# Decode intermediates and gate products move to PSUM, weight sums to GpSimd, one Strassen pair of the first MoE2 group becomes plain, and a softplus is issued later

## The chip, the core and the metric

The kernel runs on one core of one Trainium2 chip. The metric is device time of that core in microseconds (us). PE is the matrix engine (PEld its weight loads), DVE is VectorE, ACT is ScalarE, POOL is GpSimd, SP is the engine whose queue issues the DMAs.

## The reference

Sparse attention over 4 sequences of 576 tokens (8 heads of 64; half of them see the last 32 positions, half every 32nd), then two feed-forward layers over all 2304 tokens of width 512:

```python
def _moe_ref(x, w_gate, w_val, w_out):          # d_ff = 1536
    gate = 1.0 / (1.0 + np.exp(-(x @ w_gate)))
    val = x @ w_val
    return (gate * val @ w_out).astype(np.float32)

def _moe2_ref(x, w_in, w_out):                  # d_ff = 2048
    h = x @ w_in
    g = np.maximum(h, 0.0) + np.log1p(np.exp(-np.abs(h)))   # softplus
    return (g @ w_out).astype(np.float32)
```

The weights arrive as 64-bit floats, and the kernel turns them into pairs of 32-bit numbers itself.

## The kernel before

**Products.** Every 32-bit operand is held as a high and a low part, and `mm3` issues three matmuls (lines 68 to 70) for one product: high by high, high by low, low by high. Tokens lie in five blocks, four of 512 and the last (block 4) of 256. The hidden width is worked off in groups of 256 columns: six for MoE1 (groups 0 to 5), eight for MoE2 (groups 6 to 13).

**MoE1.** `step` does for one group and block: `gates` (two banks `ps_g`, sigmoid by ACT into `sg`), `out1` of the step before (four banks `ps_y`, added by DVE into `acc`, line 300), `values1` (two banks `ps_v`). When a `ps_v` is full, DVE multiplies it by `sg` (line 280), ACT rounds the product into `gh` (line 246) and DVE forms the remainder `gl` (line 247). `gh` and `gl` are what the next `out1` multiplies, and between the last `ps_v` and that `out1` stands only one `gates`.

**Decoding.** In the same steps DVE decodes pieces of 128x512 raw weights: two instructions for the high part `f` (lines 111, 115), one for the power of two `e` (line 121), one for the low word (line 133 or 191), then ACT and POOL split the result. `decode_steps` does it for MoE1's own next weights; `store_in`, `store_out` and `store_sums` do it for MoE2's weights and write them to DRAM, `store_sums` with the four differences and sums (lines 210 to 214) that the Strassen-like products need. A store passes through one of two `pair` buffers; its DMA is put into a list `ready` and issued by a later `send`. A table `plan` deals the pieces over the steps. Three `raw` buffers hold loaded pieces. `soon(n, fn)` runs `fn` after `n` more `tick`s (one per product in MoE1), and every engine works in the order in which the code was written.

**MoE2.** Blocks 0 and 1 form pair 0, blocks 2 and 3 pair 1. `pair_step` multiplies a pair with 7 products (42 matmuls) instead of 8, from operands that `operand_steps` builds of MoE1's result (differences, and their high and low parts, into `xh`/`xl` and weight buffers no longer used). After the first product A11 a copy of its bank (`snap`, line 448, ACT) must be made before A12 may add to that bank. `plain_step` does block 4 without the trick. `softplus` is three ACT instructions (lines 375 to 377), then `finish` on DVE (line 382) and the split again. `downs` are the second-layer products, six matmuls into one `ps_y`, placed between the others by `counts`. PSUM has 8 banks here: 4 for `ps_h`, `ps_g`, `ps_v`, and 4 for `ps_y`.

Of the kernel before, what the change touches and what calls it, by code (L numbers as in the profile page):

```python
# [36 lines left out]
GC = 2  # L37
# [7 lines left out]
def tile_sparse_attention_moe_moe2(  # L45
# [78 lines left out]

    def decode_steps(pools, refill=True):
        (g, m, c), low, high, f, e = fields(pools)
        hi, lo = (x[:, c * PIECE:(c + 1) * PIECE] for x in wset[g % 2][m])
        high_part(high, f)
        yield
        power(f, e)  # L130
        ff, ef = f.bitcast(F32), e.bitcast(F32)
        nc.scalar.activation(out=hi, in_=ff, func=AF.Copy)
        nc.vector.scalar_tensor_tensor(
            out=ef, in0=low, scalar=2.0 ** -52, in1=ef, op0=ALU.mult, op1=ALU.mult
        )
# [6 lines left out]
    ready, halves = [], {}  # L142
# [13 lines left out]
    def send(n=1):  # L156
        for _ in range(min(n, len(ready))):
            dst, src = ready.pop(0)
            nc.sync.dma_start(out=dst, in_=src.bitcast(F32))

    def split_store(pools, src, dst):
        pair = pools["s"].tile([P, 2, 2, HALF], F32R, tag="pair", name="pair")
        h, l = pair[:, :, 0, :], pair[:, :, 1, :]
        nc.scalar.activation(out=h, in_=src, func=AF.Copy)
        nc.gpsimd.tensor_tensor(out=l, in0=src, in1=h.bitcast(F32), op=ALU.subtract)
        ready.append((dst, pair))

    def store_in(pools):
        (g, m, c), low, high, f, e = fields(pools)
        a = pools["q"].tile([P, PIECE], F32, tag=f"a{c}", name=f"a{c}")  # L170
        nc.scalar.activation(out=a, in_=low, func=AF.Copy, scale=2.0 ** -52)
        high_part(high, f)
        yield
        power(f, e)
        load_next()
        send()
        ff, ef = f.bitcast(F32), e.bitcast(F32)
        nc.gpsimd.tensor_tensor(out=a, in0=a, in1=ef, op=ALU.mult)
        nc.gpsimd.tensor_tensor(out=a, in0=a, in1=ff, op=ALU.add)
        halves[c] = a.rearrange("p (k n) -> p k n", k=2)  # L180
        dst = in_s[g - NG1][:, 2 * c:2 * c + 2]
        soon(9, lambda: split_store(pools, halves[c], dst))
        yield

    def store_out(pools):
        (g, m, c), low, high, f, e = fields(pools)
        high_part(high, f)
        yield
        power(f, e)
        ff, ef = f.bitcast(F32), e.bitcast(F32)  # L190
        nc.vector.scalar_tensor_tensor(
            out=ef, in0=low, scalar=2.0 ** -52, in1=ef, op0=ALU.mult, op1=ALU.mult
        )
        load_next()
        send()
# [5 lines left out]
        ready.append((out_s[g - NG1][:, c], pair))  # L201
        yield

    def store_sums(pools, g, part):
# [102 lines left out]
    second = (1, 3)  # L307
    x_ops = {}

    def operand_steps(pair):  # L310
# [16 lines left out]
        def keep(name, k, src, eng):  # L327
            h, l = (x[:, k, :] for x in home[name])
            nc.scalar.activation(out=h, in_=src, func=AF.Copy)
            eng.tensor_tensor(out=l, in0=src, in1=h.bitcast(F32), op=ALU.subtract)  # L330

        for k in range(hk):
            b11, b21 = part(i, k), part(i, hk + k)
            b12, b22 = part(j, k), part(j, hk + k)
            nc.vector.tensor_tensor(out=b11, in0=b12, in1=b11, op=ALU.subtract)
            nc.gpsimd.tensor_tensor(out=b12, in0=b22, in1=b12, op=ALU.subtract)
            keep("T1", k, b11, nc.vector)
            yield
# [32 lines left out]
    def softplus(g, t, c, src, sg, pools, wait=2, last=False):  # L371
# [7 lines left out]
        soon(1, begin) if last else begin()  # L379
# [43 lines left out]
    def pair_step(g, pair, counts, pools, after=None):  # L423
# [52 lines left out]
        softplus(g, j, 0, u2, c12[:, 1, :], pools, wait=3, last=True)  # L476
# [374 lines left out]
    with tc.manual_schedule():  # L851
# [6 lines left out]
            "h": pool("ps_h2", 4, space=PSUM), "y": pool("ps_y2", 4, space=PSUM),  # L858
# [56 lines left out]
        def also(name):  # L915
            if not downs:
                next(work, None)
                next(work, None)

        for g in range(NG1, NG):  # L920
# [6 lines left out]
            first = (2, 2, 2, 2) if g > NG1 else (4, 0, 0, 0)  # L927
            if more:
                pair_step(g, 0, first, pools, also if g == NG1 else None)
                for _ in work:  # L930
                    pass
                if g > NG1:
# [86 lines left out]
```

## Time and profile before

| what | value |
|---|---|
| median of 3 runs | 1008.25 us (1006.47 to 1010.69) |
| the profiled execution | 1006.59 us, of it span 1004.8 us |
| PE busy | 936.6 us (93%) |
| DVE busy | 721.4 us (72%) |
| ACT, POOL busy | 423.2 us (42%), 320.7 us (32%) |
| mean granted PE clock | 0.97 |

Busy time of PE includes matmuls that overlap and those at a lower clock, so 93% does not say that only 7% could be saved. A share over the whole span also hides that attention, MoE1 and MoE2 have different limits; the stages are read apart below.

### The profile page before, as it was taken

The numbers are of one execution on the slowest core, as the hardware profiler recorded it, in microseconds if no ns is written. First come the engines' busy times: TensorE is split into PE (matmuls) and PEld (weight loads), VectorE is DVE, ScalarE is ACT, GpSimd is POOL, SyncE is SP. The second block draws the span as 40 slices with busy tenths as digits, with TensorE's granted clock in tenths as the row PEclk, the third lists the DMA queues.
The fourth block names the chain that finished last, engine by engine and source line by source line (L and its number), as shares of the span: only waits on it lengthen the run. The fifth ranks groups of instructions, "written<-read, shape, count | busy, mean of one in ns | idle before, by whom it ended". The sixth has DMA issues, their size and how long they took to land.

```text
span 1004.8 us, 14179 instructions
## 1 busy us (share of the span) xinstructions
PE 936.6 (93%) x5369; PEld 765.7 (76%) x5369; DVE 721.4 (72%) x1087; ACT 423.2 (42%) x815; POOL 320.7 (32%) x250
## 2 busy tenths in 40 slices
PE   8999999998997998998887996999999999999998
PEld 6777777887785886886675884878787878787886
DVE  7888665388889899889889656656665666565665
ACT  5855545232222221332133446453545454545443
POOL 4545311066555575556478644000000000000000
PEclk9999999999998998999898997999999999999999
DMA  8944321034444445443553401121212121212123
GB/s 222 238 151 141 94 80 43 1 124 129 144 158 139 147 147 167 175 139 126 179 179 142 150 1 32 53 76 51 83 44 84 42 84 43 84 42 84 43 95 136
DMA packets 39123, 107.79 MB, mean 107 GB/s; under 512 B 4752, under 2 KB 5264, under 8 KB 39056
## 3 DMA queue, kind: packets, MB, share of 16 engines
q1 hardware_dynamic: 38624, 106.28, 33.5%
q8 instruction: 42, 0.69, 0.3%
q10 hardware_dynamic: 432, 0.62, 0.2%
q14 instruction: 25, 0.20, 0.1%
HBM read 77.00 MB, written 29.88 MB: 106 GB/s over the span
## 4 chain that ended last, share of the span: by engine, by line
PE 55%; DVE 26%; ACT 10%; issue 7%; DMA 2%; POOL 0%; SPq 0%; ACTq 0%; POOLq 0%; DVEq 0%
PE ps_y L68 9%; PE ps_y L69 9%; PE ps_y L70 9%; DVE f L115 5%; DVE f L111 5%; PE ps_h L68 4%; PE ps_h L70 4%; PE ps_h L69 4%; DVE gl L247 3%; ACT gh L246 3%; DVE acc L300 2%; DVE e L121 2%; PE ps_v L68 2%; PE ps_g L68 2%; PE ps_v L70 2%
## 5 line engine op out<-in xcount | busy, mean ns | idle before, releaser
L246 ACT ACTIVATE gh<-sg 128x512 fp32r<-128x512 f32 (+1 forms) x92 | 51.0, 563 | 172.8 <-DVE sg L280 126.1
L410 DVE TENSOR_TENSOR acc<-ps_y,acc 128x512 f32<-128x512 f32 x126 | 86.1, 689 | 46.4 <-PE ps_y L70 42.5
L68 PE MATMUL ps_y<-o,gh 128*128 128x512 f32 x288 | 114.0, 396 | 0.0
L69 PE MATMUL ps_y<-o,gh 128*128 128x512 f32 x288 | 113.7, 395 | 0.0
L70 PE MATMUL ps_y<-o,gl 128*128 128x512 f32 x288 | 113.4, 394 | 0.0
L247 DVE TENSOR_TENSOR gl<-sg,gh 128x512 fp32r<-128x512 f32 (+1 forms) x92 | 72.7, 790 | 53.5 <-ACT gh L246 53.5
L115 DVE SCALAR_TENSOR_TENSOR f<-raw,f 128x512 uint32<-128x512 uint32 x68 | 81.1, 1192 | 2.3
L300 DVE TENSOR_TENSOR acc<-ps_y,acc 128x512 f32<-128x512 f32 (+1 forms) x100 | 61.0, 629 | 26.1 <-PE ps_y L70 25.9
L375 ACT ACTIVATE cs<-cs 128x512 f32<-128x512 f32 x48 | 30.3, 632 | 95.7 <-DVE cs L429 95.7
L68 PEld LDWEIGHTS ps_y<-o,gh 128*128 128x128 f32 x288 | 55.5, 193 | 11.8
L69 PEld LDWEIGHTS ps_y<-o,gh 128*128 128x128 f32 x288 | 55.3, 192 | 11.8
L70 PEld LDWEIGHTS ps_y<-o,gl 128*128 128x128 f32 x288 | 55.1, 191 | 11.7
L429 DVE TENSOR_TENSOR cs<-ps_h,cs 128x512 f32<-128x512 f32 x80 | 54.9, 686 | 11.6 <-PE ps_h L70 10.1
L68 PE MATMUL ps_y<-gh,w12h 128*128 128x512 f32 (+1 forms) x120 | 48.4, 403 | 15.6 <-ACT gh L246 15.6
L721 POOL TENSOR_TENSOR sm<-sm,st 128x480 f32<-128x480 f32 (+3 forms) x32 | 25.6, 800 | 105.9 <-DVE st L720 59.6
L111 DVE TENSOR_SCALAR f<-raw 128x512 uint32<-128x512 uint32 x68 | 58.5, 861 | 0.8 <-POOL w10l L137 0.8
L68 PE MATMUL ps_h<-xh,A 128*128 128x512 f32 (+1 forms) x128 | 44.6, 349 | 15.0 <-ACT cs L448 15.0
L68 PE MATMUL ps_y<-gh,w02h 128*128 128x512 f32 (+1 forms) x120 | 49.3, 410 | 9.8 <-ACT gh L246 9.8
L382 DVE SCALAR_TENSOR_TENSOR cs<-cs 128x512 f32<-128x512 f32 x48 | 34.1, 710 | 31.6 <-ACT cs L377 31.6
L69 PE MATMUL ps_y<-gl,w12h 128*128 128x512 f32 (+1 forms) x120 | 48.0, 400 | 4.7 <-DVE gl L247 4.6
L247 DVE TENSOR_TENSOR gl<-cs,gh 128x512 fp32r<-128x512 f32 x48 | 33.2, 691 | 26.1 <-ACT gh L246 25.9
L69 PE MATMUL ps_y<-gl,w02h 128*128 128x512 f32 (+1 forms) x120 | 48.1, 401 | 4.0 <-DVE gl L247 4.0
(194 smaller groups left out, 2600.6 us busy)
## 6 DMA issues: line engine op xcount, KB each, us to landing
raw<-in_w_dram SPq DMA_DIRECT2D x68, 512.0 KB, 4.3
in_s<-pair SPq DMA_DIRECT2D x32, 512.0 KB, 5.1
out_s<-pair SPq DMA_DIRECT2D x16, 512.0 KB, 3.9
A<-in_s SPq DMA_DIRECT2D x32, 256.0 KB, 2.8
S<-in_s SPq DMA_DIRECT2D x32, 256.0 KB, 2.7
o<-out_s SPq DMA_DIRECT2D x16, 512.0 KB, 4.3
out_dram<-acc SPq DMA_DIRECT2D x18, 256.0 KB, 2.0
qbuf<-in_q_dram SPq DMA_DIRECT2D x16, 151.0 KB, 3.1
```

The lines of the kernel that those rows point to most:

```text
L68: nc.tensor.matmul(ps, lhsT=lh, rhs=rh, start=first, stop=False, **kw)
L69: nc.tensor.matmul(ps, lhsT=lh, rhs=rl, start=False, stop=False, **kw)
L70: nc.tensor.matmul(ps, lhsT=ll, rhs=rh, start=False, stop=last, **kw)
L111: nc.vector.tensor_scalar(out=f, in0=high, scalar1=3, scalar2=0x3FFFFFFF, op0=ALU.logical_shift_left, op1=ALU.bitwise_and,)
L115: nc.vector.scalar_tensor_tensor(out=f, in0=high, scalar=0xC0000000, in1=f, op0=ALU.bitwise_and, op1=ALU.bitwise_or,)
L246: nc.scalar.activation(out=gh[:, c, 0:n], in_=src, func=AF.Copy)
L247: low = lambda: nc.vector.tensor_tensor(out=gl[:, c, 0:n], in0=src, in1=gh[:, c, 0:n].bitcast(F32), op=ALU.subtract)
L300: nc.vector.tensor_tensor(out=y, in0=ps[:, 0:n], in1=y, op=ALU.add)
L375: nc.scalar.activation(out=sg, in_=src, func=AF.Abs)
L382: nc.vector.scalar_tensor_tensor(out=sg, in0=src, scalar=0.0, in1=sg, op0=ALU.max, op1=ALU.add)
L410: nc.vector.tensor_tensor(out=y, in0=ps, in1=y, op=ALU.add)
L429: nc.vector.tensor_tensor(out=dst, in0=ps, in1=src, op=ALU.add)
```

## The change

Four edits:

- From the end of attention on, the masked word of the high part and the power of two are written to a PSUM bank `ps_x` (one buffer, taken from the `ps_y` banks, which fall from 4 to 3). In `store_in` the power stays in SBUF, because POOL reads it. The gate product overwrites its own bank `ps_v` instead of `sg`, so `gh` and `gl` are made from PSUM.
- `store_sums` runs on POOL. The DMA of a store is issued where its split is written, without `ready` and `send`; the split of the sums comes 6 ticks later instead of 2.
- In MoE2's first group (6) blocks 2 and 3 are done by two `plain_step`s with second-layer products in between. Pair 1's operands are built one piece at a time over that group, in another order, and needed from group 7 on; block 3 therefore needs its whole `xh`/`xl` (`second`).
- The softplus of block 4 starts two ticks (first half) and one tick (second half) later, which is after the next pair's A11, in the groups that have a pair behind it. The last softplus of pair 0 in front of it starts at once instead of a tick later.

The core of the diff (the new order of `operand_steps` and the removal of `send` are cut):

```diff
+    def scratch_word(pools, other):
+        if "x" not in pools:
+            return other
+        return pools["x"].tile([P, PIECE], F32, tag="x", name="ps_x").bitcast(U32)
+
-    def high_part(high, f):
+    def high_part(pools, high, f):
+        part = scratch_word(pools, f)
         nc.vector.tensor_scalar(
-            out=f, in0=high, scalar1=3, scalar2=0x3FFFFFFF,
+            out=part, in0=high, scalar1=3, scalar2=0x3FFFFFFF,
             op0=ALU.logical_shift_left, op1=ALU.bitwise_and,
         )
         nc.vector.scalar_tensor_tensor(
-            out=f, in0=high, scalar=0xC0000000, in1=f,
+            out=f, in0=high, scalar=0xC0000000, in1=part,
...
+    def low_part(pools, low, f, e):
+        x = scratch_word(pools, e)
+        power(f, x)
+        nc.vector.scalar_tensor_tensor(
+            out=e.bitcast(F32), in0=low, scalar=2.0 ** -52, in1=x.bitcast(F32),
+            op0=ALU.mult, op1=ALU.mult,
+        )
...
     def split_store(pools, src, dst):
...
-        ready.append((dst, pair))
+        nc.sync.dma_start(out=dst, in_=pair.bitcast(F32))
...
-            nc.vector.tensor_tensor(out=x, in0=a21, in1=a22, op=ALU.add)
-            nc.vector.tensor_tensor(out=y, in0=a11, in1=a21, op=ALU.subtract)
+            nc.gpsimd.tensor_tensor(out=x, in0=a21, in1=a22, op=ALU.add)
+            nc.gpsimd.tensor_tensor(out=y, in0=a11, in1=a21, op=ALU.subtract)
...
-        soon(2, lambda: split_store(pools, s, dst))
+        soon(6, lambda: split_store(pools, s, dst))
...
                     sg = sig.pop((g, t, c))[:, 0:n]
-                    nc.vector.tensor_tensor(out=sg, in0=ps[:, 0:n], in1=sg, op=ALU.mult)
-                    split_gate(g, t, c, pools, sg)
+                    prod = ps[:, 0:n]
+                    nc.vector.tensor_tensor(out=prod, in0=prod, in1=sg, op=ALU.mult)
+                    split_gate(g, t, c, pools, prod)
...
-    second = (1, 3)
+    second = (1,)
...
-    def plain_step(g, t, pools):
+    def plain_step(g, t, pools, counts=(0, 0), wait=2, after=None, reload=None):
...
-            softplus(g, t, c, ps, sg, pools)
+            softplus(g, t, c, ps, sg, pools, wait=wait, delay=GC - c if wait > 3 else 0)
+            for _ in range(counts[c]):
+                if downs:
+                    next_down(pools)
+                    tick()
+                    if after:
+                        after()
...
-            "h": pool("ps_h2", 4, space=PSUM), "y": pool("ps_y2", 4, space=PSUM),
+            "h": pool("ps_h2", 4, space=PSUM), "y": pool("ps_y2", 3, space=PSUM),
+            "x": pool("ps_x2", 1, space=PSUM),
...
-        def also(name):
-            if not downs:
-                next(work, None)
+        def also(name=None):
+            if not any(d[0] == 1 for d in downs):
                 next(work, None)
...
-                plain_step(g, NB - 1, pools)
-                fetch(g + 1, "A21", pools)
-                pair_step(g, 1, (4, 2, 2, 2), pools, reload)
+                plain_step(g, NB - 1, pools, wait=4)
+                if start:
...
+                    plain_step(g, 2, pools, (4, 1), after=also)
+                    plain_step(
+                        g, 3, pools, (3, 2), after=also, reload=lambda o: fetch(g + 1, o, pools)
+                    )
+                    for _ in work:
+                        pass
+                else:
+                    fetch(g + 1, "A21", pools)
+                    pair_step(g, 1, (4, 2, 2, 2), pools, reload)
```

How the rows of the engines move, at the three places of which the prediction speaks.

VectorE in MoE1, step of group 3 and block 0, before: a decoded piece (`f`, `e`), the adds of the block-4 `out1`, and the sums `s` from the decoded halves `a` in front of the gate product.

```order
L111 TENSOR_SCALAR f<-raw 128x512
L115 SCALAR_TENSOR_TENSOR f<-raw,f 128x512
L121 TENSOR_SCALAR e<-f 128x512
L191 SCALAR_TENSOR_TENSOR e<-raw,e 128x512
L300 TENSOR_TENSOR acc_2423<-ps_y,acc_2423 128x256 x2
L210 TENSOR_TENSOR s_3673<-a_3490 128x256
L211 TENSOR_TENSOR s_3673<-a_3451,a_3490 128x256
L300 TENSOR_TENSOR acc_2423<-ps_y,acc_2423 128x256 x2
L213 TENSOR_TENSOR s_3704<-s_3673,a_3451 128x256
L214 TENSOR_TENSOR s_3704<-a_3451,s_3704 128x256
L280 TENSOR_TENSOR sg<-ps_v,sg 128x512
L247 TENSOR_TENSOR gl<-sg,gh 128x512
```

The same place of the changed program, VectorE:

```order
L117 TENSOR_SCALAR ps_x<-raw 128x512
L121 SCALAR_TENSOR_TENSOR f<-raw,ps_x 128x512
L127 TENSOR_SCALAR ps_x<-f 128x512
L134 SCALAR_TENSOR_TENSOR e<-raw,ps_x 128x512
L301 TENSOR_TENSOR acc_2426<-ps_y,acc_2426 128x256 x4
L281 TENSOR_TENSOR ps_v<-ps_v,sg 128x512
L247 TENSOR_TENSOR gl<-ps_v,gh 128x512
```

The four sums have gone from between the adds and the gate product. They now stand on GpSimd behind the splits of the pieces (changed program, GpSimd):

```order
L200 TENSOR_TENSOR f<-f,pair 128x512
L201 TENSOR_TENSOR pair<-f,e 128x512
L211 TENSOR_TENSOR s_3720<-a_3531 128x256
L212 TENSOR_TENSOR s_3720<-a_3488,a_3531 128x256
L171 TENSOR_TENSOR pair<-s_3720,pair 128x2x256
L214 TENSOR_TENSOR s_3751<-s_3720,a_3488 128x256
L215 TENSOR_TENSOR s_3751<-a_3488,s_3751 128x256
L171 TENSOR_TENSOR pair<-s_3751,pair 128x2x256
```

ScalarE in a later MoE2 group, block 4 and the first product of pair 1, before: two softplus of three instructions, then the copy of A11's bank.

```order
L375 ACTIVATE sg<-ps_h 128x256
L376 ACTIVATE sg<-sg 128x256
L377 ACTIVATE sg<-sg 128x256
L375 ACTIVATE sg<-ps_h 128x256
L376 ACTIVATE sg<-sg 128x256
L377 ACTIVATE sg<-sg 128x256
L448 ACTIVATE cs<-ps_h 128x512
```

The changed program there (`cs` above the copy is the last softplus of pair 0):

```order
L396 ACTIVATE cs<-cs 128x512
L397 ACTIVATE cs<-cs 128x512
L398 ACTIVATE cs<-cs 128x512
L246 ACTIVATE gh<-cs 128x512
L469 ACTIVATE cs<-ps_h 128x512
L396 ACTIVATE sg<-ps_h 128x256
L397 ACTIVATE sg<-sg 128x256
L398 ACTIVATE sg<-sg 128x256
```

The copy stands in front of both softplus of block 4 now.

VectorE in the first MoE2 group, from the end of A11/A12's softplus to the sums of S3 and S1 (line 429), before; lines 335, 330 and 339 build the operands of pair 1:

```order
L247 TENSOR_TENSOR gl<-sg,gh 128x512
L335 TENSOR_TENSOR acc_65<-acc_2422,acc_65 128x512
L330 TENSOR_TENSOR xl<-acc_65,xh 128x512
L339 TENSOR_TENSOR acc_2422<-acc_2422,acc_65 128x512
L429 TENSOR_TENSOR cs<-ps_h,cs 128x512
L330 TENSOR_TENSOR w11l<-acc_2422,w11h 128x512
L429 TENSOR_TENSOR cs<-ps_h,cs 128x512
```

The changed program there:

```order
L247 TENSOR_TENSOR gl<-sg,gh 128x512
L336 TENSOR_TENSOR acc_65<-acc_2425,acc_65 128x512
L450 TENSOR_TENSOR cs<-ps_h,cs 128x512
L336 TENSOR_TENSOR acc_65<-acc_2425,acc_65 128x512
L450 TENSOR_TENSOR cs<-ps_h,cs 128x512
```

In front of the first sum stands one operand instruction instead of three, and none of those left waits for ACT.

## Rows read from the trace of the kernel before

**Rows 1.** Stage windows: busy time per engine (instructions), granted clock, DMA share, GB/s.
```profile
225.50:592.00 366.50, 334.03 (x1513) 271.90 (x1512) 312.09 (x399) 104.84 (x188) 224.93 (x154) 0.95 0.44 146
592.00:633.00 41.00, 30.66 (x135) 24.48 (x135) 23.44 (x36) 23.25 (x43) 14.65 (x13) 0.88 0.09 27
633.00:930.00 297.00, 285.60 (x1299) 236.82 (x1299) 183.10 (x289) 143.07 (x252) 0.00 (x0) 0.98 0.21 64
```

**Rows 2.** Timeline, PE: start, duration, instruction; first matmuls of some accumulations.
```profile
225.50 0.40 PE L68 MATMUL ps_g<-xh,w10h 128*128 128x512 f32 x1
...
339.24 0.28 PE L68 MATMUL ps_y<-gh,w02h 128*128 128x256 f32 x1
...
342.11 0.40 PE L68 MATMUL ps_v<-xh,w11h 128*128 128x512 f32 x1
...
374.78 0.39 PE L68 MATMUL ps_v<-xh,w11h 128*128 128x512 f32 x1
...
380.22 0.39 PE L68 MATMUL ps_g<-xh,w10h 128*128 128x512 f32 x1
...
592.20 0.40 PE L68 MATMUL ps_h<-xh,A 128*128 128x512 f32 x1
...
633.05 0.39 PE L68 MATMUL ps_h<-w10h,S 128*128 128x512 f32 x1
...
929.60 0.39 PE L68 MATMUL ps_h<-w10h,S 128*128 128x512 f32 x1
```

**Rows 3.** Waits of PE from 225 to 592: us in total, times, longest.
```profile
PE ps_y L68 <- ACT gh L246: 24.3, 14, 3.5
PE ps_y L69 <- DVE gl L247: 8.1, 13, 1.3
```

**Rows 4.** Waits of PE from 592 to 633.
```profile
PE ps_h L68 <- DVE cs L429: 6.7, 2, 3.9
PE ps_h L68 <- ACT cs L448: 3.6, 2, 3.4
```

**Rows 5.** Waits of PE from 633 to 930.
```profile
PE ps_h L68 <- ACT cs L448: 11.4, 6, 1.9
```

**Rows 6.** Groups of VectorE from 225 to 592, by form: busy, mean ns, idle before.
```profile
L115 DVE SCALAR_TENSOR_TENSOR f<-raw,f 128x512 uint32<-128x512 uint32 x51 | 68.3, 1340 | 1.7
L111 DVE TENSOR_SCALAR f<-raw 128x512 uint32<-128x512 uint32 x50 | 47.6, 952 | 0.0
...
L247 DVE TENSOR_TENSOR gl<-sg,gh 128x512 fp32r<-128x512 f32 x34 | 34.3, 1009 | 26.2 <-ACT gh L246 26.2
L121 DVE TENSOR_SCALAR e<-f 128x512 uint32<-128x512 uint32 x51 | 29.6, 580 | 0.7
...
L214 DVE TENSOR_TENSOR s<-a,s 128x256 f32<-128x256 f32 x8 | 8.2, 1029 | 0.3
...
L211 DVE TENSOR_TENSOR s<-a,a 128x256 f32<-128x256 f32 x8 | 6.6, 821 | 0.0
```

**Rows 7.** Single lines from 225 to 592: shortest, median, longest ns.
```profile
L115 DVE SCALAR_TENSOR_TENSOR f<-raw,f x51: 691/1661/1669, 224.9 to 537.6; 128x512 uint32<-128x512 uint32 x51
...
L300 DVE TENSOR_TENSOR acc<-ps_y,acc x84: 407/678/693, 241.9 to 589.5; 128x512 f32<-128x512 f32 x68, 128x256 f32<-128x256 f32 x16
...
L165 POOL TENSOR_TENSOR pair<-s,pair x16: 1272/1294/1482, 254.5 to 552.9; 128x512 fp32r<-128x512 f32 x16
```

**Rows 8.** Waits of ScalarE from 225 to 592.
```profile
ACT gh L246 <- DVE sg L280: 95.7, 35, 8.3
ACT pair L198 <- DMA out_s<-pair: 21.8, 4, 7.6
```

**Rows 9.** Timeline around the copy of one later group, ScalarE and then PE.
```profile
671.76 0.37 ACT L375 ACTIVATE sg<-ps_h 128x256 f32<-128x256 f32 x1
...
674.10 0.58 ACT L448 ACTIVATE cs<-ps_h 128x512 f32<-128x512 f32 x1
...
674.73 0.50 PE L68 MATMUL ps_h<-xh,A 128*128 128x512 f32 x1 [1.90 <-ACT cs L448]
```

More of the change, by code (lines that the diff above doesn't have):

```diff
@@ L127, in decode_steps @@
         hi, lo = (x[:, c * PIECE:(c + 1) * PIECE] for x in wset[g % 2][m])
-        high_part(high, f)
+        high_part(pools, high, f)
         yield
-        power(f, e)
         ff, ef = f.bitcast(F32), e.bitcast(F32)
         nc.scalar.activation(out=hi, in_=ff, func=AF.Copy)
-        nc.vector.scalar_tensor_tensor(
-            out=ef, in0=low, scalar=2.0 ** -52, in1=ef, op0=ALU.mult, op1=ALU.mult
-        )
+        low_part(pools, low, f, e)
         pools["e"].tensor_tensor(out=ff, in0=ff, in1=hi.bitcast(F32), op=ALU.subtract)
@@ L140, in decode_steps @@
         yield
-    ready, halves = [], {}
+    halves = {}
     late_q = deque()
@@ L154, in tick @@
                 item[1]()
[L156 to L159, printed above, removed]
     def split_store(pools, src, dst):
@@ L175, in store_in @@
         load_next()
-        send()
         ff, ef = f.bitcast(F32), e.bitcast(F32)
@@ L186, in store_out @@
         (g, m, c), low, high, f, e = fields(pools)
-        high_part(high, f)
+        high_part(pools, high, f)
         yield
-        power(f, e)
+        low_part(pools, low, f, e)
         ff, ef = f.bitcast(F32), e.bitcast(F32)
-        nc.vector.scalar_tensor_tensor(
-            out=ef, in0=low, scalar=2.0 ** -52, in1=ef, op0=ALU.mult, op1=ALU.mult
-        )
         load_next()
-        send()
         pair = pools["s"].tile([P, 2, PIECE], F32R, tag="pair", name="pair")
@@ L200, in store_out @@
         nc.gpsimd.tensor_tensor(out=lo, in0=ff, in1=ef, op=ALU.add)
-        ready.append((out_s[g - NG1][:, c], pair))
+        nc.sync.dma_start(out=out_s[g - NG1][:, c], in_=pair.bitcast(F32))
         yield
@@ L369, in product, with softplus @@
             )
-    def softplus(g, t, c, src, sg, pools, wait=2, last=False):
+    def softplus(g, t, c, src, sg, pools, wait=2, delay=0):
         n = blocks[t][1]
@@ L377, in begin @@
             nc.scalar.activation(out=sg, in_=sg, func=AF.Ln, bias=1.0)
-        soon(1, begin) if last else begin()
+        soon(delay, begin) if delay else begin()
         def finish():
@@ L421, in add_downs, with pair_step @@
             downs.extend((2, g, t, u) for u in range(blocks[t][1] // P))
-    def pair_step(g, pair, counts, pools, after=None):
+    def pair_step(g, pair, counts, pools, after=None, delay=1):
         i, j = 2 * pair, 2 * pair + 1
@@ L475, in pair_step @@
         plus(u2, Dk, u2)
-        softplus(g, j, 0, u2, c12[:, 1, :], pools, wait=3, last=True)
+        softplus(g, j, 0, u2, c12[:, 1, :], pools, wait=2 + delay, delay=delay)
         add_downs(g, i, pools)
         add_downs(g, j, pools)
-    def plain_step(g, t, pools):
+    def plain_step(g, t, pools, counts=(0, 0), wait=2, after=None, reload=None):
         n = blocks[t][1]
@@ L927, in tile_sparse_attention_moe_moe2 @@
             first = (2, 2, 2, 2) if g > NG1 else (4, 0, 0, 0)
+            start = g == NG1
             if more:
[L929 to L932, printed above, removed]
+                pair_step(g, 0, first, pools, also if start else None, 0)
+                if not start:
                     fetch_out(g, pools)
-                plain_step(g, NB - 1, pools)
-                fetch(g + 1, "A21", pools)
-                pair_step(g, 1, (4, 2, 2, 2), pools, reload)
+                plain_step(g, NB - 1, pools, wait=4)
+                if start:
+                    for name in OPS[NCC:]:
+                        fetch(g + 1, name, pools)
+                    plain_step(g, 2, pools, (4, 1), after=also)
[7 more added lines that the diff above has]
+                    pair_step(g, 1, (4, 2, 2, 2), pools, reload)
             else:
```

57 lines of the change are left out of this document (38 added, 19 removed).

## The prediction

> **What bounds the kernel now.** I read the stage windows first, to see where PE, the engine with the most work, stands still or slow; then PE's waits in each such stage; then the engine waited for. Attention and the first MoE1 steps (to 225.50) and the last group (from 929.60) I leave as they are: the edits hardly touch them. The rest falls into three stretches, and in each I compare the time taken with the time that the same matmuls take undisturbed. The yardstick is in the timeline: the 24 matmuls of 512 columns from 374.78 to 380.22 take 5.44 us, 0.2267 each; the 24 of 256 columns from 339.24 to 342.11 take 2.87 us, 0.1196 each [rows 2].
>
> - A, MoE1 from 225.50 to 592.20: 366.7 us. By the loops it holds 17 steps' gates and values and 17 `out1` of 512-token blocks (17x48 + 17x24 = 1224 matmuls) and 4x48 + 4x24 = 288 of 256 columns: 277.5 + 34.4 = 311.9. **54.8 us are lost.** PE waits 32.4 of them, at the start of `out1` on `gh` (24.3) and `gl` (8.1) [rows 3]; most of the rest is the clock: the stretch was granted 0.95 [rows 1], and the lower level (1.2 instead of 2.4 GHz) follows PE's idle time.
> - B, MoE2's first group to its S3 of pair 1, 592.20 to 633.05: 40.85 us for 84 matmuls of 512 and 48 of 256 columns, 24.8. **16.1 us lost**, 10.3 of them waits: DVE's sums `cs` 6.7, ACT's copy 3.6 [rows 4]. The clock was 0.88 [rows 1].
> - C, six groups from 633.05 to 929.60: 296.55 us for 6 x (192 + 24 matmuls) = 6 x 46.39 = 278.3. **18.2 lost**, of which 11.4 is one wait, once per group, for the copy on line 448 [rows 5].
>
> Why A waits: `gh` waits for DVE's product 95.7 us in all, up to 8.3 at a time [rows 8]. DVE is busy 312.1 of 366.5 us there [rows 1]; it is late, not idle. Its instructions are long because POOL works too: line 115 takes 0.691 at its shortest and 1.661 in the median, while line 300, as wide but with one operand in PSUM, has median 0.678 and never exceeds 0.693 [rows 7]. ACT adds to it: it stands up to 7.6 us before a `pair` buffer whose DMA has not landed [rows 8], with `gh` queued behind.
>
> **The change, term by term.** *PSUM operands (A).* No row shows DVE writing PSUM. Bounds: the cheapest row without interference is 0.41 (line 300's shortest, of the 256-column form), the dearest is line 115's 1.67 [rows 7]. I take line 300's 0.69, since it is as wide and touches PSUM. Line 115: 51 x (1.34 - 0.69) = 33.1 us less. Line 111: 50 x (0.952 - 0.69) = 13.1 less. Line 121 moves in 37 of its 51 uses, mean 0.58, so 4 us more. Line 247 (512 columns): 34 x (1.009 - 0.69) = 10.8 less [rows 6].
>
> The Trainium skill (SBUF — State Buffer, "Who interferes with whom") says that a VectorE instruction with at most one SBUF input and outside the two-port modes does not contend with GpSimd; lines 115 and 300 of this trace agree. By that rule alone the sum below stays as it is. Against the change speaks VectorE: DVE Perf Modes, "Mode 2×_2P": an fp32 single-source instruction runs at double rate only from SBUF to SBUF. By that rule lines 111 and 121 lose their fast form, and the price of 0.69 above already is the slow one.
>
> *Sums (A).* 32 instructions leave DVE; the dearest line has mean 1.029, the cheapest 0.821, 8 each [rows 6]: 26 to 33, say 30 us. In sum DVE sheds 33 + 13 - 4 + 11 + 30 = 83 of 312 us. POOL gains 32 of half the width of line 165's 1.29 [rows 7], 0.65 each, 21 us on 225 [rows 1]. If A takes 327 us, DVE is busy 229 (70%) and POOL 246 (75%).
>
> *Stores (A).* A DMA issued with its split lands sooner, which frees `pair` and shortens the waits of [rows 8]. But SP now stands at a store until POOL has written the low part, and the next `raw` load stands behind it; with three `raw` buffers a load has about two pieces' time in hand, so I cost it at nothing except where POOL is late. That is group 5, blocks 0 and 1: three input pieces (9 POOL instructions), four output pieces (8), four sums (4 splits, 8 half-width) and four `xl` of `out1`: 25 x 1.29 + 8 x 0.65 = 37.5 us in two steps of 72 x 0.2267 = 16.3, 32.6 together. POOL ends 4.9 late, and ACT, which waits for POOL's `a` and `s` and for `pair`, holds `gh` behind it.
>
> *What stays lost in A.* Behind block 4's gates `out1` has only 2.87 us for product and `gl` (0.69 each at most, as line 300), `gh` (about 0.6, as the copy in [rows 9], as wide and from PSUM too) and at worst one half piece of 2 x 0.69: 3.35, four times 0.5. Group 5: 4.9 late in each of two steps, less what the 5.44 us of gates cover; I put 8. One `ps_y` bank fewer: the fourth `ps_y` of an `out1` now waits for the first add, which has 2 x 1.36 = 2.7 us (block 4: 1.4); a half piece fits before the first, not always before the second: 2. With the lower clock behind each wait, 15. From nothing (0) to half the present loss (27): **A gains 40, from 28 to 55.**
>
> *First group (B).* Before the first sum stands one operand instruction instead of three, none with ACT's step between: S3 ends, DVE does 0.69 + 0.69 while PE has S1 (6 x 0.2267 = 1.36), so A22 and S4 wait little; I leave 2 of the 16.1. T2 and the late copy of pair 1 are not needed in this group any more. The plain pair has 48 matmuls for 42: 6 x 0.2267 = 1.4 more. The moved operand pieces lie beside 48 + 60 matmuls, 24 us. The loads of group 7 go out during the plain steps and are needed over 5 us later. **B gains 12.7, from 0 to 14.7.**
>
> *Softplus (C).* Now the six instructions of block 4 end at 674.10 and only then comes the copy; PE starts A12 1.90 later than it could [rows 9]. With the copy in front it is done 0.58 after A11, and PE has S2 (1.36) in between. Behind the copy then stand the softplus of block 4 and A's; their `finish` on DVE comes four ticks later, under four second-layer products (5.4 us). The clock's share goes with the waits. I leave 1: **C gains 17.2, from 11.4 to 18.2.**
>
> Sum: 40 + 12.7 + 17.2 = 69.9. The profiled execution had span 1004.8 and 1006.59 in all, 1.8 around the span and 1.7 below the median of the runs. 1004.8 - 69.9 + 1.8 = 936.7, so **937 us**; its own range is 918 (all three at their best: 1006.6 - 88) to 950.
>
> **Rivals.**
> 1. POOL and the two `pair` buffers become the bound of A: ACT stands before POOL as it stood before DVE. For it: the 37.5 us above, and ACT's waits on stores. Against it: outside group 5 POOL has a quarter free. A gains 25: 952 us.
> 2. The change doesn't do what it says in A: a PSUM operand spares DVE nothing, because a write to PSUM waits like one to SBUF. For it: no row has such a write. Against it: line 300. Then only the sums leave, 30 of 312 us, and A gains about 18: 959 us.
> 3. B and C give their gains back, the wait for the copy being replaced by one for DVE's `finish` in front of the first sum: 1006.6 - 40 = 967 us. For it: that `finish` stands in front of it in DVE's queue. Against it: between them lie four second-layer products.
> 4. Slower: `raw` loads behind the stores. 48 stores stand in SP's queue; if each held the next load so long that DVE and then PE stood still by 1.5 us, that is 72 us and eats the gain: 1009 us; beyond 1.6 each it is slower by over 0.5%. Against it: a store would have to wait longer than two pieces, some 8 us, and the present loads never stop DVE, whose line 111 has no idle time before it [rows 6].
>
> **How the numbers follow.** Forecast 0.62, rival 1 0.22, rival 2 0.08, rival 3 0.05, rival 4 0.03. A range from 918 to 963 holds the first three, less the outer edges. About 0.5% (5 us) is what a measurement of this kernel can tell from no change; only rival 4 comes near it, so faster 0.95, same 0.02, slower 0.03.
>
> **What would show it.** Right: lines 117, 121, 127 and 134 of the changed kernel and 247 in MoE1 near 0.69 with narrow spread while POOL works; DVE's busy time in MoE1 about 80 us lower; PE's waits for `gh` a quarter; one stretch of full clock there; no wait for the copy (line 469) in the later groups, whose period is 46.4 us; no wait for T2. Wrong: medians above 1 us on these lines (rival 2); waits of ACT for `pair` or `s` with `gh` behind them (rival 1); DVE idle before line 117 until a `raw` DMA lands (rival 4); waits of PE for `ps_y` adds, which I cost at 2 us.

## The result, and the profile after

The changed kernel takes **939.86 us** (median of 4 runs, 939.08 to 941.92) against 1008.09 (1006.47 to 1010.69) for the kernel before on the same chip: ratio 0.932, interval 0.930 to 0.935. The forecast was 937, with a range from 918 to 963. The profiled execution took 939.08 us with a span of 937.3, so 67.5 us less span than before; the sum of the prediction was 69.9.

From the page of the changed kernel: the span; PE's busy time; the granted clock in 40 slices, which shows 9, the highest digit, in every slice; and the chain of work that ended last. This chain is followed back only to 417.57 us, so its shares add up to 55% of the span and say nothing of the part before: 41 of the 55 are PE's, 5 DVE's.

```profile
span 937.3 us, 14185 instructions
...
PE 910.2 (97%) x5375; PEld 753.3 (80%) x5375; DVE 629.9 (67%) x1050; ACT 423.7 (45%) x816; POOL 318.4 (34%) x284
...
PEclk9999999999999999999999999999999999999999
...
PE 41%; DVE 5%; ACT 5%; DMA 2%; issue 1%; POOL 1%; SPq 0%; ACTq 0%; DVEq 0%; POOLq 0%
```

The stage windows of the changed kernel, for stretches A, for B with the first part of C, and for the next five periods of C (columns as in [rows 1]):

```profile
223.50:544.60 321.10, 315.17 (x1513) 264.79 (x1512) 228.68 (x363) 105.07 (x187) 222.21 (x186) 0.99 0.48 167
544.60:624.20 79.60, 74.79 (x357) 61.10 (x357) 51.97 (x79) 46.08 (x84) 14.10 (x13) 1.00 0.17 53
624.20:862.50 238.30, 233.56 (x1082) 194.14 (x1081) 151.90 (x240) 119.28 (x210) 0.00 (x0) 1.00 0.21 67
```

By the starts of PE's accumulations the span divides like this:

| stretch | before | after | gained | forecast |
|---|---|---|---|---|
| start to A | 225.50 | 223.40 | 2.1 | 0 |
| A, MoE1 | 366.70 | 321.25 | 45.45 | 40 |
| B, and one period of C | 91.07 | 79.51 | 11.6 | 12.7 + 2.9 |
| five periods of C | 246.33 | 238.34 | 8.0 | 14.3 |
| the last group | 75.2 | 74.8 | 0.4 | 0 |

The third row cuts C one period late, where both kernels show the same place (S3 of pair 1 in group 7), so B stands there with one of C's six periods. A is 9.35 us longer than its matmuls undisturbed (311.9), where 54.8 were lost before; the forecast left 15.

The groups of DVE in A after the change (busy us, mean ns of one, idle before). They answer to [rows 6]:

```profile
L121 DVE SCALAR_TENSOR_TENSOR f<-raw,ps_x 128x512 uint32<-128x512 uint32 x50 | 34.4, 688 | 5.2
L117 DVE TENSOR_SCALAR ps_x<-raw 128x512 uint32<-128x512 uint32 x50 | 34.4, 687 | 10.1 <-DMA raw<-in_w_dram 9.7
...
L281 DVE TENSOR_TENSOR ps_v<-ps_v,sg 128x512 f32<-128x512 f32 x34 | 23.7, 696 | 14.7 <-PE ps_v L70 14.7
L247 DVE TENSOR_TENSOR gl<-ps_v,gh 128x512 fp32r<-128x512 f32 x34 | 23.5, 692 | 26.7 <-ACT gh L246 26.7
L127 DVE TENSOR_SCALAR e<-f 128x512 uint32<-128x512 uint32 x14 | 7.1, 505 | 0.2
```

Single lines (shortest, median, longest ns, and for line 117 what its engine stood for), which answer to [rows 7]; first line 111 of the kernel before, whose place line 117 takes, then three of the changed kernel:

```profile
L111 DVE TENSOR_SCALAR f<-raw x50: 410/920/1524, 228.6 to 536.6; 128x512 uint32<-128x512 uint32 x50
```

```profile
L117 DVE TENSOR_SCALAR ps_x<-raw x50: 681/684/695, 222.4 to 494.8; 128x512 uint32<-128x512 uint32 x50
...
  DMA raw<-in_w_dram: 9.7, 7
...
L121 DVE SCALAR_TENSOR_TENSOR f<-raw,ps_x x50: 686/687/691, 223.2 to 495.6; 128x512 uint32<-128x512 uint32 x50
...
L171 POOL TENSOR_TENSOR pair<-s,pair x16: 1272/1294/1554, 244.3 to 509.4; 128x512 fp32r<-128x512 f32 x16
```

The lines that now touch PSUM take 0.69 us with hardly any spread, while POOL is busy 222 of the 321 us: line 117 lies between 0.681 and 0.695, where line 111 lay between 0.410 and 1.524, and line 121 between 0.686 and 0.691, where line 115 lay between 0.691 and 1.669 [rows 7]. POOL's split (line 171) has the median of before, 1.29. DVE's busy time in A went from 312.1 to 228.7 us: 83.4 less, forecast 83.

PE's waits in A after the change, which answer to [rows 3], and then in the five periods of C, which answer to [rows 5]:

```profile
PE ps_y L68 <- DVE acc L301: 5.3, 3, 3.2
PE ps_y L68 <- ACT gh L246: 0.4, 1, 0.4
PE ps_y L69 <- DVE gl L247: 0.2, 1, 0.2
```

```profile
PE ps_h L68 <- ACT cs L469: 4.7, 5, 0.9
```

The waits for `gh` and `gl`, 32.4 us before, are 0.6. What is left in A is three waits for a `ps_y` bank, and one of them, of 3.2, lies in a step that stands out: `out1` of group 5, block 1, lasts 11.43 us where its 24 matmuls need 5.44. This is its timeline (all engines; SPq is SP's queue of DMA issues):

```profile
483.36 0.66 ACT L177 ACTIVATE a<-raw 128x512 f32<-128x512 uint32 x1 [5.25 <-POOL s L215]
...
484.62 1.28 POOL L171 TENSOR_TENSOR pair<-s,pair 128x512 fp32r<-128x512 f32 x1 [1.29 <-ACT pair L170]
...
485.93 0.32 SPq L172 DMA_DIRECT2D in_s<-pair  x1
...
486.35 0.37 SPq L99 DMA_DIRECT2D raw<-in_w_dram  x1
...
490.37 0.69 DVE L117 TENSOR_SCALAR ps_x<-raw 128x512 uint32<-128x512 uint32 x1 [2.77 <-DMA raw<-in_w_dram]
...
491.78 0.68 DVE L301 TENSOR_TENSOR acc<-ps_y,acc 128x512 f32<-128x512 f32 x1
...
492.52 0.79 PE L68 MATMUL ps_y<-gh,w12h 128*128 128x512 f32 x1 [3.25 <-DVE acc L301]
```

It is read from the top. ACT stands 5.25 us for POOL's sum before it can take line 177, which reads a `raw` piece and ends at 484.02. By the order of the program the next load goes into the buffer of this piece. POOL's split of a pair (171) ends at 485.90, and SP's store of it goes out at 485.93. The load stands behind that store in SP's queue: 486.35, 2.3 us after its buffer was free. DVE stands 2.77 us for this load, so its first add comes only at 491.78; the fourth `ps_y` of the step needs the bank which that add frees, and PE stands 3.25. Behind that wait the clock stood at its lower level, 0.50 of full speed, and the matmul takes 0.79 where 0.39 is usual. The window of the rest of this step (columns as above):

```profile
492.50:495.20 2.70, 2.68 (x6) 2.15 (x7) 2.24 (x4) 1.89 (x3) 2.70 (x4) 0.50 0.68 256
```

In C one wait of 0.95 per group is left. The timeline of one group, PE, DVE and ACT:

```profile
661.73 0.40 PE L68 MATMUL ps_h<-xh,A 128*128 128x512 f32 x1
...
663.00 0.69 DVE L403 SCALAR_TENSOR_TENSOR cs<-cs 128x512 f32<-128x512 f32 x1 [2.03 <-ACT cs L398]
663.10 0.39 PE L68 MATMUL ps_h<-w11h,S 128*128 128x512 f32 x1
...
663.72 0.63 ACT L246 ACTIVATE gh<-cs 128x512 fp32r<-128x512 f32 x1 [0.76 <-DVE cs L403]
...
664.26 0.58 ACT L469 ACTIVATE cs<-ps_h 128x512 f32<-128x512 f32 x1
...
664.89 0.50 PE L68 MATMUL ps_h<-xh,A 128*128 128x512 f32 x1 [0.95 <-ACT cs L469]
```

PE starts A11 at 661.73 and S2 at 663.10; the copy (line 469) could have run after A11, from about 663.1. It runs at 664.26, since `gh` of pair 0's last softplus (line 246) stands in front of it in ACT's queue and waits 0.76 for DVE's `finish` (line 403).

### The profile page after: what moved, and what is told of

It reads as the page before. It is cut to its first block, busy times and chain, and to the rows that moved or that the text cites. A ratio compares the mean times of both kernels' runs of the same rounds, so it can differ in the third digit from the quotient of the medians.

```text
span 937.3 us, 14185 instructions
## 1 busy us (share of the span) xinstructions
PE 910.2 (97%) x5375; PEld 753.3 (80%) x5375; DVE 629.9 (67%) x1050; ACT 423.7 (45%) x816; POOL 318.4 (34%) x284
## 4 chain that ended last, share of the span: by engine, by line
PE 41%; DVE 5%; ACT 5%; DMA 2%; issue 1%; POOL 1%; SPq 0%; ACTq 0%; DVEq 0%; POOLq 0%
PE ps_y L68 8%; PE ps_y L70 8%; PE ps_y L69 8%; PE ps_h L68 4%; PE ps_h L70 4%; PE ps_h L69 4%; DMA raw<-in_w_dram 2%; ACT gh L246 1%; DVE cs L403 1%; DVE gl L247 1%; PE ps_v L70 1%; PE ps_v L68 1%; PE ps_v L69 1%; DVE cs L450 1%; ACT cs L396 1%
## 5 line engine op out<-in xcount | busy, mean ns | idle before, releaser
L68 PE MATMUL ps_y<-o,gh 128*128 128x512 f32 x288 | 112.2, 389 | 0.2 <-ACT gh L246 0.2
L69 PE MATMUL ps_y<-o,gh 128*128 128x512 f32 x288 | 112.1, 389 | 0.0
L246 ACT ACTIVATE gh<-ps_v 128x512 fp32r<-128x512 f32 (+1 forms) x60 | 33.3, 556 | 121.2 <-DVE ps_v L281 119.3
L247 DVE TENSOR_TENSOR gl<-ps_v,gh 128x512 fp32r<-128x512 f32 (+1 forms) x60 | 38.3, 638 | 41.4 <-ACT gh L246 41.4
L70 PEld LDWEIGHTS ps_y<-o,gl 128*128 128x128 f32 x288 | 54.1, 188 | 12.7 <-DVE gl L247 1.4
L68 PEld LDWEIGHTS ps_y<-o,gh 128*128 128x128 f32 x288 | 54.1, 188 | 11.7 <-ACT gh L246 0.6
L69 PEld LDWEIGHTS ps_y<-o,gh 128*128 128x128 f32 x288 | 54.1, 188 | 11.2
L450 DVE TENSOR_TENSOR cs<-ps_h,cs 128x512 f32<-128x512 f32 x75 | 51.4, 686 | 10.9 <-PE ps_h L70 9.4
L68 PE MATMUL ps_h<-xh,A 128*128 128x512 f32 (+1 forms) x140 | 48.6, 347 | 6.6 <-ACT cs L469 6.5
L281 DVE TENSOR_TENSOR ps_v<-ps_v,sg 128x512 f32<-128x512 f32 (+1 forms) x60 | 38.5, 642 | 23.3 <-PE ps_v L70 23.1
L267 ACT ACTIVATE sg<-ps_g 128x512 f32<-128x512 f32 (+1 forms) x60 | 32.8, 552 | 38.4 <-PE ps_g L70 28.4
L69 PE MATMUL ps_h<-xl,A 128*128 128x512 f32 (+1 forms) x140 | 47.8, 342 | 0.0
L70 PE MATMUL ps_h<-xh,A 128*128 128x512 f32 (+1 forms) x140 | 47.8, 341 | 0.0
L68 PE MATMUL ps_y<-gh,w02h 128*128 128x512 f32 (+1 forms) x120 | 45.9, 382 | 1.5 <-ACT acc L299 1.2
```

The lines of the kernel that those rows point to most:

```text
L68: nc.tensor.matmul(ps, lhsT=lh, rhs=rh, start=first, stop=False, **kw)
L69: nc.tensor.matmul(ps, lhsT=lh, rhs=rl, start=False, stop=False, **kw)
L70: nc.tensor.matmul(ps, lhsT=ll, rhs=rh, start=False, stop=last, **kw)
L246: nc.scalar.activation(out=gh[:, c, 0:n], in_=src, func=AF.Copy)
L247: low = lambda: nc.vector.tensor_tensor(out=gl[:, c, 0:n], in0=src, in1=gh[:, c, 0:n].bitcast(F32), op=ALU.subtract)
L267: nc.scalar.activation(out=sg[:, 0:n], in_=ps[c][:, 0:n], func=AF.Sigmoid)
```

## The experiments

Two theories were set against each other. **D**: DVE's long instructions set A, and PSUM operands make them short. **S**: the stores issued at once set it, because `pair` comes free sooner and ACT no longer stands with `gh` behind it. Differences in us below are those of the ratios to the kernel before, times 1008; each has some 2 us of doubt. Stage lengths are from one profile each; the four kernels whose MoE1 is that of the changed kernel (it, u_late, u_plain and copy_first) have A from 320.2 to 322.7, and the step that stands out from 10.21 to 11.54. "End" is from the end of A to the last matmul: 408.5 us before, 388.9 after.

**u_scratch: the scratch of the decoding back in SBUF.** All else as in the changed kernel; its bank stays unused.

```diff
-        if "x" not in pools:
-            return other
-        return pools["x"].tile([P, PIECE], F32, tag="x", name="ps_x").bitcast(U32)
+        return other
```

> The decode's masked word and power of two are in SBUF again; all else as changed (3 ps_y banks, too). Theory D (MoE1 was lost to VectorE instructions that GpSimd lengthens): the two instructions of the high part go back to medians of 0.9 and 1.6 us, VectorE is busy some 45 us more in MoE1 and about half of the 45 us gained there goes: 955 to 965 us. Theory S (MoE1 was lost to ScalarE standing before store buffers, cured by issuing the stores' DMAs at once): PE does not notice, 940 to 943 us.

974.69 us (973.36 to 975.12), ratio 0.968 (0.966 to 0.970): 35.5 slower than the changed kernel, more than D's figure. A takes 355.5. DVE's two lines of the upper part in A, and PE's wait for the adds:

```profile
L119 DVE SCALAR_TENSOR_TENSOR f<-raw,f 128x512 uint32<-128x512 uint32 x51 | 72.2, 1416 | 1.7
L115 DVE TENSOR_SCALAR f<-raw 128x512 uint32<-128x512 uint32 x50 | 48.3, 967 | 4.3 <-DMA raw<-in_w_dram 3.1 <-POOL pair L169 1.2
```

```profile
PE ps_y L68 <- DVE acc L299: 25.9, 8, 5.0
```

The lines are long again. But PE now stands for `ps_y`, not for `gh`: with three banks a late DVE stops PE at the adds. How much of the 35 us is that bank?

**scratch4: the same, with the bank given back to `ps_y`.**

```diff
-            "h": pool("ps_h2", 4, space=PSUM), "y": pool("ps_y2", 3, space=PSUM),
-            "x": pool("ps_x2", 1, space=PSUM),
+            "h": pool("ps_h2", 4, space=PSUM), "y": pool("ps_y2", 4, space=PSUM),
```

> The decode's scratch is in SBUF as in the first experiment, and ps_y has its fourth bank back. If that experiment's 35 us are VectorE's longer instructions by themselves: 968 to 976 us. If a good part is the missing bank, in front of which PE waited 25.9 us there: 948 to 962 us.

968.16 us (966.86 to 969.69), ratio 0.961 (0.960 to 0.963), A 351.9. PE's waits in A:

```profile
PE ps_y L68 <- ACT gh L244: 16.0, 10, 2.3
PE ps_y L69 <- DVE gl L245: 1.6, 7, 0.2
```

PE waits for `gh` again, as before the change. So of u_scratch's 35 us, 29 remain with the bank given back, and 6 go with the missing bank. That bank counts for more when DVE is late: PE's wait for the adds is 25.9 in u_scratch and 5.3 in the changed kernel, with three banks in both.

**psum_alone: the kernel before with the PSUM operands and the gate product in PSUM only** (three `ps_y` banks, sums on DVE, stores by the old list, softplus and first group as before).

```diff
+    def scratch_word(pools, other):
...
+        return pools["x"].tile([P, PIECE], F32, tag="x", name="ps_x").bitcast(U32)
...
-                    nc.vector.tensor_tensor(out=sg, in0=ps[:, 0:n], in1=sg, op=ALU.mult)
-                    split_gate(g, t, c, pools, sg)
+                    prod = ps[:, 0:n]
+                    nc.vector.tensor_tensor(out=prod, in0=prod, in1=sg, op=ALU.mult)
+                    split_gate(g, t, c, pools, prod)
```

> The kernel before with nothing but the PSUM operands (decode scratch and gate product, three ps_y banks); sums, stores, first group and softplus as before. If these operands carry nearly all of the 45 us of MoE1: 960 to 966 us. If the sums or the stores carry a third of it: 970 to 980 us.

962.95 us (962.73 to 964.74), ratio 0.957 (0.955 to 0.958): 43.7 of the 68 us. A takes 325.7, so 41 of the 45.45 gained there; the end, 408.0, is that of before. ACT's waits for a `pair` buffer are still there (A, two rows):

```profile
ACT pair L206 <- DMA out_s<-pair: 22.6, 4, 8.4
...
ACT pair L206 <- DMA in_s<-pair: 15.9, 5, 7.4
```

A is 4.5 us longer than in the changed kernel, so these waits and the other edits that are missing here cost no more than that once DVE is quick. That speaks against S.

**u_send: the list of stores again.**

```diff
-        nc.sync.dma_start(out=dst, in_=pair.bitcast(F32))
+        ready.append((dst, pair))
```

(The calls of `send` come back with it.)

> The stores' DMAs are put on the list and issued by a later send again. Theory S: ScalarE stands before pair buffers some 40 us again, and most of the gain in MoE1 goes: 960 to 985 us. Theory D: some 0 to 6 us are lost to ScalarE's waits, but the raw loads no longer stand behind stores, so VectorE's waits for raw (9.7 us) fall under 2: 937 to 946 us.

936.78 us (936.48 to 938.01), ratio 0.931 (0.929 to 0.932); A 318.8. ACT's waits in A:

```profile
ACT pair L206 <- DMA out_s<-pair: 22.4, 4, 8.4
ACT pair L206 <- DMA in_s<-pair: 18.6, 5, 8.1
ACT a L182 <- POOL s L222: 17.7, 3, 6.7
```

The long waits for `pair` are back, and the kernel is no slower. S falls. It is quicker by 1.7 us, and the intervals of the two overlap. DVE's waits for `raw` in A, 9.7 before, are gone, as D said.

**u_gate: the gate product back in SBUF.**

```diff
-                    nc.vector.tensor_tensor(out=prod, in0=prod, in1=sg, op=ALU.mult)
-                    split_gate(g, t, c, pools, prod)
+                    nc.vector.tensor_tensor(out=sg, in0=ps[:, 0:n], in1=sg, op=ALU.mult)
+                    split_gate(g, t, c, pools, sg)
```

> The gate product is in SBUF again. Theory D: the remainder gl takes up to 1.7 us again, mean about 1.0 instead of 0.69, some 11 us of VectorE in MoE1, on the way to the second-layer product, but with idle time of gates before it: 941 to 947 us. Theory S: 940 us.

947.83 us (946.28 to 950.84), ratio 0.942 (0.939 to 0.944): 9.5 slower, a little above what was expected. A takes 328.1 and begins at 228.10 instead of 223.40: 6.8 in A and 4.7 ahead of it. Not all of the 4.7 is this edit: 2.5 of it are lost ahead of 50 us, before the first gate product (56.51), and 1.8 between 50 and 100 us. Line 247 in A:

```profile
L247 DVE TENSOR_TENSOR gl<-sg,gh 128x512 fp32r<-128x512 f32 x34 | 36.1, 1061 | 28.5 <-ACT gh L246 28.5
```

**u_sums: the four sums on DVE again.**

```diff
-            nc.gpsimd.tensor_tensor(out=x, in0=a21, in1=a22, op=ALU.add)
+            nc.vector.tensor_tensor(out=x, in0=a21, in1=a22, op=ALU.add)
```

(and so for the other three)

> The weight sums are on VectorE again (their split still 6 ticks later, DMAs issued at once). Theory D: about 28 us more on VectorE in MoE1: 944 to 952 us. Against it, if GpSimd being late in MoE1's last group costs the 6 us lost at the step of group 5 and block 1, that loss goes: 934 to 938 us. Theory S: 940 us.

940.0 us (939.56 to 940.41), ratio 0.934 (0.932 to 0.935): no difference. D's figure is missed, and so is the other, by which the loss of group 5 goes; the 940 is S's. The window of A, and PE's wait for the adds in it:

```profile
223.30:544.80 321.50, 315.24 (x1515) 263.72 (x1514) 251.89 (x395) 104.53 (x187) 200.70 (x154) 1.00 0.49 167
```

```profile
PE ps_y L68 <- DVE acc L301: 4.6, 5, 2.0
```

DVE has 23 us more and POOL 22 less than in the changed kernel, and A is as long. But inside A things have moved: the `out1` of group 5, block 1, takes 7.23 instead of 11.43, as ACT doesn't stand for POOL's sums any more; the next one takes 7.30 instead of 5.44, and the other steps lose 5.9 instead of 3.3 (3.3 to 5.2 in the four kernels with one MoE1). The sums gain a little where POOL has room and lose it where POOL is late.

**u_late: the softplus of block 4 as before**, the copy behind it, and pair 0's last softplus as before, too.

```diff
-        softplus(g, j, 0, u2, c12[:, 1, :], pools, wait=2 + delay, delay=delay)
+        softplus(g, j, 0, u2, c12[:, 1, :], pools, wait=3, delay=1)
...
-                plain_step(g, NB - 1, pools, wait=4)
+                plain_step(g, NB - 1, pools)
```

> Block 4's softplus and pair 0's last softplus are issued as before the change. If the copy's wait behind block 4's softplus is what was cured, PE waits 1.9 us per later group again instead of 0.9: 945 to 951 us (6 or 7 times 0.95, up to 1.75 with the lower clock that followed). If the later groups gained for another reason (fewer banks, other order of loads), 939 to 941 us.

950.03 us (947.48 to 950.95), ratio 0.944 (0.942 to 0.946): 11.7 slower, the end 397.2. PE's wait for the copy, whole stretch:

```profile
PE ps_h L68 <- ACT cs L469: 12.3, 7, 1.9
```

**u_plain: the pair in the first group again**, with the new order of its operands (the diff in short).

```diff
-    second = (1,)
+    second = (1, 3)
...
-                    plain_step(g, 2, pools, (4, 1), after=also)
...
+                fetch(g + 1, "A21", pools)
+                pair_step(g, 1, (4, 2, 2, 2), pools, reload)
```

> Blocks 2 and 3 of MoE2's first group are a pair again, with pair 1's operands built inside pair 0 (in the changed kernel's order of steps). If the plain pair is what gained: PE waits for the sums and for T2 again, 947 to 952 us. If the new order of the operand steps alone gained: 939 to 943 us, or 1.4 less for the six matmuls saved.

951.57 us (948.21 to 955.46), ratio 0.946 (0.943 to 0.949): 13.7 slower, the end 399.0. PE's waits in the first group:

```profile
PE ps_h L68 <- DVE cs L450: 8.1, 2, 5.5
PE ps_h L68 <- ACT cs L469: 4.5, 1, 4.5
```

They are of the kind of [rows 4], the first with up to 5.5 at a time. The run takes back the pair and, with it, the place of its operand steps inside pair 0; which of the two makes the waits is not separated.

**copy_first: pair 0's last softplus finishes one tick later**, so that its `gh` does not stand before the copy.

```diff
-        softplus(g, j, 0, u2, c12[:, 1, :], pools, wait=2 + delay, delay=delay)
+        softplus(g, j, 0, u2, c12[:, 1, :], pools, wait=3, delay=delay)
```

> The finish of pair 0's last softplus comes one tick later, so that the copy of A11's bank stands in front of its gh on ScalarE. If that gh is what still holds the copy 0.95 us in each later group: the wait goes, the period falls from 47.7 to about 46.4 us, 931 to 934 us. If the copy is held by something else, or the finish then stands in front of the first sum, 939 to 943 us.

932.39 us (931.97 to 932.87), ratio 0.927 (0.926 to 0.928): 5.6 quicker than the changed kernel, 6.7 by the spans. The period of C is 46.42. PE's waits for `cs` from 544 to 930:

```profile
PE ps_h L68 <- DVE cs L450: 1.7, 2, 1.4
PE ps_h L68 <- ACT cs L469: 0.8, 1, 0.8
```

**spread: three pieces of group 5's crowded first steps decoded earlier.** Groups 2 to 4 each take one more of the MoE2 pieces in their first step; group 5 takes 4 and 4 in its first two steps instead of 6 and 5.

```diff
-        extra = 1 if i < 4 else (3, 2, 2, 2, 2)[t] if g < NG1 - 1 else (6, 5, 0, 0, 0)[t]
+        extra = 1 if i < 4 else (4, 2, 2, 2, 2)[t] if g < NG1 - 1 else (4, 4, 0, 0, 0)[t]
```

> The plan gives MoE1's groups 2 to 4 one more store piece each (four at block 0) and the last group 4 and 4 instead of 6 and 5. If the 6 us lost at group 5, block 1 come from GpSimd being late there, with loads and ScalarE behind it: 933 to 936 us. If the pieces only carry the loss into earlier groups: 939 to 945 us.

933.36 us (932.42 to 934.2), ratio 0.928 (0.927 to 0.930): 4.3 quicker, 6.6 by the spans; A 314.7. PE's waits and DVE's for `raw` in A:

```profile
PE ps_y L68 <- DVE acc L301: 2.0, 1, 2.0
```

```profile
DVE ps_x L117 <- DMA raw<-in_w_dram: 1.3, 2, 0.7
```

**copy_and_spread: both edits together.**

```diff
+        softplus(g, j, 0, u2, c12[:, 1, :], pools, wait=3, delay=delay)
...
+        extra = 1 if i < 4 else (4, 2, 2, 2, 2)[t] if g < NG1 - 1 else (4, 4, 0, 0, 0)[t]
```

> The later finish and the spread plan together. They act in different stretches, so their gains of 7 and 6 us should add: 925 to 928 us. If the faster start only moves a wait: 930 us or more.

926.76 us (924.11 to 927.98), ratio 0.921 (0.919 to 0.923): 11.8 quicker than the changed kernel, where the two alone gave 5.6 and 4.3. The sum of the two, 9.9, is within the doubt of the three figures. A 314.3, the end 380.8.

**all_three: the two lines of copy_and_spread, and the list of stores of u_send.**

```diff
+        ready.append((dst, pair))
```

> The two together, with the stores' DMAs issued later by send. If send gained by letting the raw loads go ahead of late stores in group 5, the spread plan has already taken that: within 1.5 us of the two alone, 924 to 928 us. If it helps elsewhere too: 921 to 924 us.

924.55 us (923.88 to 926.71), ratio 0.918 (0.917 to 0.920): an interval that overlaps with that of the two alone, so nothing is shown for the stores here either. It is the quickest version of this study.

## Why the prediction was right, point by point

- **PSUM operands: right, in mechanism and price.** The price taken, 0.69, measured 0.687 (line 117), 0.688 (121) and 0.692 (247); rival 2 (a write to PSUM as dear as one to SBUF) falls by the same rows. The trace agrees with the rule cited from the Trainium skill (SBUF — State Buffer, "Who interferes with whom"): with one SBUF input left, the spread of line 117 is 14 ns and that of line 121 is 5 ns beside a busy POOL. It agrees with the other, too (the Trainium skill, VectorE: DVE Perf Modes, "Mode 2×_2P"): line 117, which writes to PSUM, has lost the quick form, 0.681 at its shortest where line 111 had 0.410. By psum_alone these edits alone are worth 44 us; by u_scratch, scratch4 and u_gate A gets longer by 7 to 34 us without them.
- **Sums: no net term of the gain.** They cost DVE 30 us by the rows of before and 23 in u_sums, and u_sums shows no time for them: DVE is at 78% of A with the sums (251.89 of 321.5), and A is as long. This is a balance: with the sums on DVE the crowded step of group 5 is 4.2 shorter, and others are longer. A's gain was worked out from what stays lost and not from the 83, so the forecast wasn't hurt by it. What the sums' move would bring while DVE is still late was not run.
- **What stays lost in A: 9.35 us, forecast 15.** The mis-sized term was this residue. Group 5 was the right place (8 forecast, 6.0 in one step), by both mechanisms named there: ACT behind POOL (rival 1) and a load behind a store in SP's queue (rival 4). Neither spreads: rival 4's other 1.5 us per store do not appear; DVE stands for `raw` 9.7 us in 7 places in all. By spread, fewer pieces in group 5 (less work there for DVE, ACT, POOL and the DMAs alike) take A to 314.7 and the wait for `raw` to 1.3. Two runs take one mechanism away each. With the old list (u_send) no load stands behind a late store; the step lasts 8.78 us instead of 11.43 and the next one 1.1 more. With the sums off POOL (u_sums) it lasts 7.23 and the next one 1.9 more. So both mechanisms are at work; as the step alone varies by 1.3 from profile to profile, their shares of the 6.0 are not settled. Block 4's half-pieces and the second add (2 + 2 forecast) can be no more than the two other waits for `ps_y`, 2.1 us together.
- **Ahead of A: 2.1 us that were not forecast.** "The edits hardly touch them", said of the steps ahead of A, was wrong: MoE1's first steps run among attention's and use the gate product too. By the starts of PE's accumulations 1.6 of the 2.1 lie ahead of 182 us, among attention's matmuls. psum_alone has the 2.1 as well (A from 223.41). Between 50 and 100 us, the kernel before and u_gate, the two with the product in SBUF, lose 1.8 us each against the changed kernel, and no other run loses any; in that stretch lie the first gate products.
- **First group (B): right in mechanism, too high in size.** 15.6 forecast with one period of C, 11.6 gained; 1.8 of the 4 missing is the next point's wait (in copy_first the same stretch takes 77.67). PE still waits 1.7 for DVE's sums (copy_first's row). u_plain has the waits of [rows 4] back with the pair and its operand steps.
- **Softplus (C): the mechanism right, one step wrong.** Five periods gained 8.0 of 14.3; the period is 47.67, forecast 46.4. The failing step is "With the copy in front it is done 0.58 after A11": pair 0's last `gh` stands in front of the copy and waits for DVE, so PE waits 0.95, and its next matmul takes 0.50 for 0.39; what remains of the 1.28 per group was not traced further, but it goes with the wait: copy_first has the period of 46.42. u_late shows that the two softplus moves together are worth 8 to 12 us.
- **Rivals.** 3 (B and C give their gains back) falls by the table: 20 us of the 67.5 are theirs. 1 and 4 exist at one place and cost 6 us there (4.8 to 6.1 in the four kernels with one MoE1).

The errors went both ways: A gave 5.5 more than forecast, the stretch before it 2.1, C and B gave 10.3 less; so 67.5 came out beside 69.9. That the sum is so close is luck.

## What to carry to other kernels

When an in-order engine is late because another engine makes its instructions long, look first for operands that can lie elsewhere (here one PSUM bank as scratch and the gate product left in its bank): that was worth 44 us, while moving whole instructions off the engine brought no net gain once it was no longer late, and made the engine that took them late in the busiest step. For each instruction on which the next engine waits, list what stands in front of it in its own queue and for what that in turn waits, the queue of DMA issues included: a wait of 0.76 us for a `finish` cost 5.6 us over the groups by the runs. A buffer given away costs more where its reader is late (6 us in u_scratch; in the changed kernel PE waits 5.3 us in all for the three banks left, 3.2 of them behind a late load), so free the reader first.

## What the runs showed of the hardware that was not expected

- DVE writes PSUM, 128x512 of 4 bytes, as quickly and as steadily as it reads it: 0.681 to 0.695 over the 50 of line 117, 0.686 to 0.691 over the 50 of line 121.
- POOL gained from the change too: it is busy 222.2 us in A, though 32 sums came to the 224.9 of before (246 forecast). Its instructions had been drawn out beside DVE's, as DVE's were beside POOL's: with the scratch back in SBUF (u_scratch), POOL is busy 247.6 in A. One of them in A, of the kernel before and then of the changed one (here line 147); in u_scratch its mean is 1.627 again:

```profile
L136 POOL TENSOR_TENSOR f<-f,w12h 128x512 f32<-128x512 f32 x4 | 6.7, 1664 | 8.0 <-DVE e L121 4.4 <-ACT w12h L132 3.5
```

```profile
L147 POOL TENSOR_TENSOR f<-f,w12h 128x512 f32<-128x512 f32 x4 | 5.2, 1296 | 4.0 <-DVE ps_x L127 4.0
```

- A half-width sum on POOL (128x256) takes 0.74, not half of the 1.29 that most of its full-width instructions take.
- The clock follows the waits: with them gone the granted clock is 0.99 in A and 1.00 in B and C ([rows 1]: 0.95, 0.88, 0.98). Behind the wait of 3.25 in A it was 0.50; behind the one of 0.95 shown for C (664.8 to 666.3) it was 1.00.
